# Key transposes of odd blocks moved to partitions 64 to 127 and issued in turn with the query transposes

## The chip, the cores and the metric

One core of one Trainium2 chip runs the kernel. The metric is the device time of one execution in microseconds; the time before is 1073.29 us, the median of three runs (1073.01 to 1078.38 us).

## The reference, cut to what matters

Three layers follow one another: attention over chunks, a feed-forward layer with a smooth activation, and a mixture of eight experts with one expert per token. The change touches the attention alone. Each chunk of 32 queries sees 8 memory keys, 16 keys to its left, its own 32 and 8 to its right:

```python
batch, n_heads, seq, head_dim = (4, 8, 768, 64)
for c in range(nc):
    q_c = q[:, :, c_start:c_end]
    k_ctx = k[:, :, l_start:r_end]
    k_full = np.concatenate([mem_k, k_ctx], axis=2)
    scores = scale * np.matmul(q_c, k_full.transpose(0, 1, 3, 2))
    ...
    out[:, :, c_start:c_end] = np.matmul(a, v_full)
```

The scores contract over the head dimension, so queries and keys have to lie with the head dimension on the partitions. They arrive from memory with the position on the partitions, and TensorE transposes them.

## The kernel before, in words

The attention is cut into 48 blocks of 64 queries and all 8 heads (u = 0 to 47, 12 blocks to a sequence). Blocks 0 to 17 are made by `blocks`, blocks 18 to 47 by `chunks` (line 1600, `BY_CHUNK` = 18). Blocks go in pairs that share one tile of transposed keys, kT. The even block of a pair loads its 64 queries and 96 keys (8 of memory, 24 of context, 64). The odd block loads 64 queries and the 64 keys that the even one has not brought.

For a block, the load (`load_qk`, lines 544 to 557) puts queries in qn, partitions 0 to 63, and keys in kn, from partition 0 on. The job T (lines 581 to 592) then makes eight transposes on TensorE, each of two heads (128 columns): first four of the queries into the PSUM tile p_qT (line 586), then four of the keys into the PSUM tile p_kT (line 588). p_qT and p_kT are two of three buffers of one tag, "a". The jobs qT and kT (lines 594 to 603) copy them to SBUF on ScalarE or VectorE, S (lines 605 to 617) makes the scores, and the softmax, PT (transposes of the weights), V (weights times values, lines 654 to 663) and the copies xh and xl follow.

The feed-forward layer runs at the same time: step s of `mlp` has a job mm_h (line 748, twelve matmuls) and a job mm_y (line 794, nine matmuls), with a chain of ScalarE and VectorE operations between them. Attention blocks are slipped in between these jobs, ahead of the feed-forward steps that need them. After the last rows the experts' stage follows (lines 1342 to 1522).

The order of the work is not written out by hand. Every job states its engines with a cost in ns (`job`, line 117), what it comes after and which buffers it takes, and `Plan.order` (lines 136 to 195) plays the program through on these costs: at each step it takes, among the jobs that could begin within `SLACK` = 34 ns of the earliest, the one of lowest rank. The engines then run the order so found, each its own queue in sequence. The cost of T on TensorE stands in line 683:

```python
job(("T", u), T, {E: 560 if odd else 630}, rank=R(0), after=[("qk", u)], ...
```

The loads are issued by SyncE (SP) in its own planned order; qn and kn have one buffer each, so a block's load waits for the T of the block before it.

Of the kernel before, what the change touches and what calls it, by code (L numbers as in the profile page):

```python
# [9 lines left out]
F32 = mybir.dt.float32  # L10
# [9 lines left out]
B, H, S, D = 4, 8, 768, 64  # L20
NMEM = 8
CHUNK, LEFT, RIGHT = 32, 16, 8
QB = 64
CTX = QB + LEFT + RIGHT
NK = CTX + NMEM
# [85 lines left out]
class Plan:  # L111
# [5 lines left out]
    def job(self, key, fn, on, rank, after=(), get=(), use=(), lat=130, tiled=False):  # L117
        uses = list(use) + [h for _, h in get]
        for h in uses:
            self.users.setdefault(h, []).append(key)  # L120
        for _, h in get:
            self.getter[h] = key
        self.jobs[key] = dict(fn=fn, on=on, rank=rank, after=list(after), get=list(get), use=list(use), lat=lat, tiled=tiled,
                              need=[(tag, sum(t == tag for t, _ in get)) for tag in dict(get)])
# [91 lines left out]
def attn_moe_moe_kernel(ctx, tc, q, k, v, mem_k, mem_v, w_in, w_out, emb, tau, w1, w2, cst, out, ydbg=None):  # L216
    nc = tc.nc
# [5 lines left out]
    ident = cf[:, 0:128]  # L223
# [10 lines left out]
    att = pa.enter_context(tc.tile_pool(name="att", bufs=1))  # L234
# [8 lines left out]
    def psa(shape, name):  # L243
        return ps_a.tile(shape, F32, tag="a", name=name)
# [3 lines left out]
    job, A, V_, G, E = plan.job, "Activation", "DVE", "Pool", "PE"  # L248
    engs = {A: nc.scalar, V_: nc.vector, G: nc.gpsimd}
    xt, yp = {}, {}  # L250
    tl = {}
# [278 lines left out]
    def chunks(u):  # L530
        b, i = divmod(u, NQB)
        j, o = divmod(u, SPB)
        R = lambda x: x + (1.4 * u - 17.5 if u < (LEAVE + 1) * SPB else 2 * o + 32 if j == LEAVE + 1 else 8 * u / 3 - 20.4)
        J = H // 2
        odd, pair = u % 2, u // 2
        w = QB * i - LEFT
        edge = 0 if i == 0 else 1 if i == NQB - 1 else None
        new = QB if odd else NMEM + PREV + QB
# [4 lines left out]

        def load_qk(e):
            qn = tl["qn", u] = att.tile([QB, H, D], F32, tag="qn", bufs=1, name="qn")
            kn = tl["kn", u] = att.tile([NK, H, D], F32, tag="kn", bufs=1, name="kn")
            get = lambda n, x, lo, hi: nc.sync.dma_start(out=kn[n:n + hi - lo], in_=x[b, :, lo:hi, :].rearrange("h p d -> p h d"))
            nc.sync.dma_start(out=qn, in_=q[b, :, i * QB:(i + 1) * QB, :].rearrange("h p d -> p h d"))
            if not odd:
                get(0, mem_k, 0, NMEM)  # L550
            lo, hi = w + (PREV if odd else 0), w + PREV + QB
            n = 0 if odd else NMEM
            if lo < 0:
                get(n, k, 0, -lo)
            if hi > NQB * QB:
                get(n + NQB * QB - lo, k, 0, hi - NQB * QB)
            get(n + max(-lo, 0), k, max(lo, 0), min(hi, NQB * QB))
# [23 lines left out]
        def T(e):  # L581
            p1 = psa([128, J, QB], "p_qT")
            p2 = psa([128, J, new], "p_kT")
            a, c = tl["qn", u], tl["kn", u]
            for n in range(J):
                nc.tensor.transpose(p1[:, n, :], a[:, 2 * n:2 * n + 2, :].rearrange("p h d -> p (h d)"), ident[:QB, :QB])
            for n in range(J):
                nc.tensor.transpose(p2[:, n, :], c[0:new, 2 * n:2 * n + 2, :].rearrange("p h d -> p (h d)"), ident[:new, :new])
            tl["T", u] = p1, p2
            tl["qT", u] = att.tile([128, J, QB], F32, tag="qT", name="qT")  # L590
            if not odd:
                tl["kT", pair] = att.tile([128, J, 5 * GR - NMEM], F32, tag="kT", name="kT")
# [78 lines left out]
        def x_lo(e):  # L671
# [4 lines left out]
        prev = lambda x: [(x, u - 1)]  # L676
        mem = 4 if u < BY_CHUNK + 2 or i < 2 else 0
        plan.dma(("qk", u), load_qk, dict(SP=470 * ((2 if odd else 3) + (edge is not None))), (QB + new) * 4e3, R(-4), [("issue", "qk", u - 1)], [(t, (t, u)) for t in ("qn", "kn")])
        plan.dma(("v", u), load_v, dict(SP=470 * (8 + mem + (2 if edge is not None else 0))), 4 * SEEN * 2e3, R(0), [("issue", "v", u - 1)], [("vn", ("vn", u))])
        t1, t2 = ("a", u, 1), ("a", u, 2)  # L680
        pss, pr, mxh, sm = ("pS", u), ("pr", u), ("mx", u), ("sm", u)
        kt, xb = ("kT", pair), [("X", u), ("X2", u)]
        job(("T", u), T, {E: 560 if odd else 630}, rank=R(0), after=[("qk", u)], use=[(t, u) for t in ("qn", "kn")] + ([kt] if odd else []),
            get=[("a", t1), ("a", t2), ("qT", ("qT", u))] + ([] if odd else [("kT", kt)]))
        job(("qT", u), qT, {A: 264, V_: 330}, rank=R(1), after=[("T", u)], use=[t1, ("qT", u)])
        job(("kT", u), kT, {A: 264, V_: 330} if odd else {A: 371 + 210, V_: 465 + 200}, rank=R(1), after=[("T", u)], use=[t2, kt])
# [253 lines left out]
    def routing():  # L940
# [51 lines left out]
        def group(g):  # L992
# [203 lines left out]
            for x, (j0, j1) in enumerate(chunks):  # L1196
                h = ("rhs", g, x)
                sh = [128, j1 - j0, ns]
                wd = 60 + (j1 - j0) * ns
                cc = slice(j0, j1)  # L1200

                def ids(e, x=x, sh=sh, cc=cc, h=h):
                    if g == 2:
                        p = gp if ctag[x][0] == "g" else mp
                        t = r[h] = p.tile([128, CH, 6, ns], BF16, tag=ctag[x], bufs=1 if x > 5 else 2, name="rhs2")
                    else:
                        t = r[h] = r["rhs1"][x]
                    V.tensor_tensor(t[:, :, 0, :], mid(slots[g], sh), last(r["z"][:, cc], sh), ALU.is_equal)

                key = ("ids", g, x)  # L1210
                job(key, ids, {V_: wd}, rank=rk, after=[k3] + ([("mm_y", KFF * NBLK - 1)] if g == 2 else []), use=every,
                    get=[(ctag[x], h)] if g == 2 else [])
                us = [h] if g == 2 else []
                ch.append((j0, j1, h, us))
                last_ids.append(steps([
                    ({V_: wd}, lambda e, h=h: e.tensor_scalar(r[h][:, :, 1, :], r[h][:, :, 0, :], part, None, ALU.mult)),
                    ({V_: wd}, lambda e, h=h, sh=sh, cc=cc: e.tensor_tensor(r[h][:, :, 2, :], r[h][:, :, 0, :], last(tiles[:, cc], sh), ALU.mult)),
                ], [key], rk, us))
                last_gates.append(steps([
                    ({V_: wd}, lambda e, h=h, m=m, sh=sh, cc=cc: e.tensor_tensor(r[h][:, :, 3 + m, :], r[h][:, :, 0, :], last(r["gb"][m][:, cc], sh), ALU.mult))  # L1220
                    for m in range(3)
                ], [last_ids[-1], gate], rk + (2 if g == 1 else 30), us))
# [376 lines left out]
    for u in range(NSUB):  # L1599
        (blocks if u < BY_CHUNK else chunks)(u)  # L1600
# [7 lines left out]
    for kind, n in TURNS:  # L1608
        c = FIRST + 2 * n
# [50 lines left out]
```

## Time and profile before

| | us |
|---|---|
| median of three runs | 1073.29 |
| the profiled execution | 1077.64 |
| its span, first to last instruction | 1075.9 |
| TensorE busy | 1044.6 |
| VectorE busy | 751.5 |
| ScalarE busy | 692.2 |
| GpSimd busy | 168.0 |

The profiled execution is 4.35 us above the median. The span is what the rows of the trace divide up; the profiled execution's time is 1.74 us longer than it. PE stands for TensorE's matmuls, PEld for its weight loads, which can run beside matmuls; a transpose is a weight load of the data and a matmul with the identity. DVE is VectorE, ACT is ScalarE, SP is SyncE. A row of the timeline merges neighbouring instructions of one line: start, length from the first start to the last end, count. The ends of matmuls are modelled, so starts say more than ends.

### The profile page before, as it was taken

The numbers are of one execution on the slowest core, as the hardware profiler recorded it, in microseconds if no ns is written. First come the engines' busy times: TensorE is split into PE (matmuls) and PEld (weight loads), VectorE is DVE, ScalarE is ACT, GpSimd is POOL, SyncE is SP. The second block draws the span as 40 slices with busy tenths as digits, with TensorE's granted clock in tenths as the row PEclk, the third lists the DMA queues.
The fourth block names the chain that finished last, engine by engine and source line by source line (L and its number), as shares of the span: only waits on it lengthen the run. The fifth ranks groups of instructions, "written<-read, shape, count | busy, mean of one in ns | idle before, by whom it ended". The sixth has DMA issues, their size and how long they took to land. (4 is left out here: it accounts for less than half of the span.)

```text
span 1075.9 us, 22578 instructions
## 1 busy us (share of the span) xinstructions
PE 1044.6 (97%) x8404; PEld 912.3 (85%) x8404; DVE 751.5 (70%) x1607; ACT 692.2 (64%) x1617; POOL 168.0 (16%) x109
## 2 busy tenths in 40 slices
PE   8899999999999999999999999998999999999996
PEld 6678888998888888888888889888899888988995
DVE  5999996556756566556556556886978657777851
ACT  4888887777757777777777777855633444443441
POOL 0000100000000000000000000010135645655552
PEclk9899999999999999999999999998999999999998
DMA  7966540032331112112112100019459877568200
GB/s 192 258 195 183 160 128 23 1 101 62 97 80 40 41 41 60 40 43 61 41 40 70 28 17 31 1 27 378 173 188 399 292 227 250 170 216 268 88 30 22
DMA packets 164019, 128.09 MB, mean 119 GB/s; under 512 B 106229, under 2 KB 135285, under 8 KB 163647
## 3 DMA queue, kind: packets, MB, share of 16 engines
q1 hardware_dynamic: 159439, 111.63, 34.4%
q0 software_dynamic: 4464, 14.95, 3.9%
q8 instruction: 69, 1.13, 0.4%
q14 instruction: 47, 0.39, 0.1%
HBM read 119.19 MB, written 16.52 MB: 126 GB/s over the span
## 5 line engine op out<-in xcount | busy, mean ns | idle before, releaser
L748 PE MATMUL p_h<-xt,win_h 128*128 128x384 f32 x1024 | 273.3, 348 | 1.7 <-DVE rn L777 1.5
L748 PEld LDWEIGHTS p_h<-xt,win_h 128*128 128x128 f32 x1024 | 183.0, 190 | 9.4 <-DVE rn L777 3.2
L748 PE MATMUL p_h<-xt,win_l 128*128 128x384 f32 x512 | 174.2, 340 | 0.0
L767 DVE SCALAR_TENSOR_TENSOR m<-sq,rn 128x384 f32<-128x384 f32 x128 | 71.8, 561 | 123.1 <-ACT rn L256 122.4
L794 PE MATMUL p_y<-wout_h,gh 128*128 128x512 f32 x384 | 155.9, 406 | 0.5 <-DVE gh L266 0.5
L266 ACT CAST ehi<-eraw 128x1024 fp32r<-128x1024 f32 x89 | 92.8, 1048 | 98.5 <-PE p_y L1496 51.5
L1378 DVE TENSOR_TENSOR elo<-eraw,ehi 128x1024 fp32r<-128x1024 f32 x89 | 125.6, 1419 | 42.6 <-ACT ehi L266 35.8
L794 PE MATMUL p_y<-wout_h,gl 128*128 128x512 f32 x384 | 151.8, 395 | 0.0
L794 PE MATMUL p_y<-wout_l,gh 128*128 128x512 f32 x384 | 151.4, 394 | 0.0
L1496 PE MATMUL p_y<-ehi,hh 128*128 128x512 f32 x432 | 142.1, 398 | 1.0 <-DVE hh L1465 1.0
L1406 PE MATMUL p_h<-xs,ehi 128*128 128x256 f32 x704 | 129.5, 285 | 0.0
L752 ACT ACTIVATE sq<-p_h 128x384 f32<-128x384 f32 x128 | 62.4, 488 | 78.4 <-PE p_h L748 78.0
L1406 PEld LDWEIGHTS p_h<-xs,ehi 128*128 128x128 f32 x704 | 111.0, 191 | 1.6 <-DVE xs L1359 0.4
L1378 POOL TENSOR_TENSOR elo<-eraw,ehi 128x1024 fp32r<-128x1024 f32 x39 | 96.9, 2484 | 79.8 <-ACT ehi L266 51.7
L1406 PE MATMUL p_h<-xs,elo 128*128 128x256 f32 x352 | 100.4, 285 | 0.0
L771 ACT ACTIVATE m<-m,few 128x384 f32<-128x384 f32 x128 | 79.1, 618 | 32.1 <-DVE m L767 31.2
L1300 POOL DMA_INDIRECT vn<-y_d,gi x27 | 27.6, 1023 | 453.3 <-DVE si L1247 402.7
L1496 PEld LDWEIGHTS p_y<-ehi,hh 128*128 128x128 f32 x432 | 81.1, 188 | 19.6 <-DVE hh L1465 2.3
L748 PEld LDWEIGHTS p_h<-xt,win_l 128*128 128x128 f32 x512 | 97.0, 190 | 0.0
L794 PEld LDWEIGHTS p_y<-wout_h,gl 128*128 128x128 f32 x384 | 72.2, 188 | 17.7 <-DVE gl L785 0.4
L1496 PE MATMUL p_y<-elo,hh 128*128 128x512 f32 x216 | 85.3, 395 | 0.0
L774 DVE SCALAR_TENSOR_TENSOR rn<-m,rn 128x384 f32<-128x384 f32 x128 | 70.8, 553 | 20.4 <-ACT m L771 19.1
(285 smaller groups left out, 1872.3 us busy)
## 6 DMA issues: line engine op xcount, KB each, us to landing
eraw<-in_moe_w_dram SPq DMA_DIRECT2D x128, 512.0 KB
raw<-in_moe_w_in_dram SPq DMA_DIRECT2D x16, 512.0 KB
raw<-in_moe_w_out_dram SPq DMA_DIRECT2D x16, 512.0 KB
y_d<-ysb SPq DMA_DIRECT2D x24, 256.0 KB
qn<-in_q_dram SPq DMA_DIRECT2D x43, 128.0 KB
vn<-in_v_dram SPq DMA_DIRECT2D x114, 32.0 KB
vn<-in_v_dram SPq DMA_DIRECT2D x122, 24.0 KB
kn<-in_k_dram SPq DMA_DIRECT2D x22, 128.0 KB
```

Of the source, the lines that this page charges most:

```text
L266: (nc.scalar.copy if e == A else nc.vector.tensor_copy)(out, src)
L748: nc.tensor.matmul(p, w, xt[j][:, a, kk, :], start=(n == 0), stop=(n == len(ops) - 1))
L752: nc.scalar.activation(t, tl["h", s], AF.Tanh, scale=0.5)
L767: nc.vector.scalar_tensor_tensor(t, tl["sq", s], 4.0, tl["rn", s], ALU.add, ALU.mult)
L771: nc.scalar.activation(t, t, AF.Square, bias=c15)
L774: nc.vector.scalar_tensor_tensor(tl["rn", s], tl["m", s], 0.75, tl["rn", s], ALU.add, ALU.mult)
L794: nc.tensor.matmul(yp[yh][t], x[:, c], w[g][:, o, :], start=(first and n == 0), stop=(final and n == 2))
L1300: nc.gpsimd.indirect_dma_start(out=tl["xg", u, a], out_offset=None, in_=y_d[0:T1 * 128, :] if g == 1 else y_d[:, :], in_offset=bass.Indire ...
L1378: engs[e].tensor_sub(tl["elo", j], raw[b, second, c], tl["ehi", j].bitcast(F32))
L1406: nc.tensor.matmul(p[:, o, :], w[:, kk, s], v[:, kk, :], start=(kk == 0 and m == 0), stop=(kk == KDM - 1 and m == 2))
L1496: nc.tensor.matmul(tl["yy", u][a], v[:, kk, s], w[:, k, :], start=(kk == 0 and m == 0), stop=(kk == KEF - 1 and m == 2))
```

## The change

In `chunks`, that is for blocks 18 to 47: the keys of odd blocks are loaded to partitions 64 to 127 of kn (which now has 128 partitions instead of 96), and their transposes read them there, with that corner of the identity. The two loops over transposes become one, so that queries and keys take turns, in odd blocks and in even blocks alike; the keys of even blocks stay where they were. The planner's cost of T in odd blocks goes from 560 to 330 ns; that in even blocks stays at 630.

```diff
-            kn = tl["kn", u] = att.tile([NK, H, D], F32, tag="kn", bufs=1, name="kn")
+            kn = tl["kn", u] = att.tile([128, H, D], F32, tag="kn", bufs=1, name="kn")
...
-            n = 0 if odd else NMEM
+            n = QB if odd else NMEM
...
             a, c = tl["qn", u], tl["kn", u]
+
+            r = slice(QB, QB + new) if odd else slice(0, new)
             for n in range(J):
                 nc.tensor.transpose(p1[:, n, :], a[:, 2 * n:2 * n + 2, :].rearrange("p h d -> p (h d)"), ident[:QB, :QB])
-            for n in range(J):
-                nc.tensor.transpose(p2[:, n, :], c[0:new, 2 * n:2 * n + 2, :].rearrange("p h d -> p (h d)"), ident[:new, :new])
+                nc.tensor.transpose(p2[:, n, :], c[r, 2 * n:2 * n + 2, :].rearrange("p h d -> p (h d)"), ident[r, r])
...
-        job(("T", u), T, {E: 560 if odd else 630}, rank=R(0), ...
+        job(("T", u), T, {E: 330 if odd else 630}, rank=R(0), ...
```

## Rows read from the trace of the kernel before

**Rows 1.** The page: busy time by engine; TensorE's busy tenths and granted clock.

```profile
PE 1044.6 (97%) x8404; PEld 912.3 (85%) x8404; DVE 751.5 (70%) x1607; ACT 692.2 (64%) x1617; POOL 168.0 (16%) x109
...
PE   8899999999999999999999999998999999999996
...
PEclk9899999999999999999999999998999999999998
```

**Rows 2.** Windows: stretch, length, busy by engine (instructions), PEclk, DMA share, GB/s.

```profile
150.00:615.00 465.00, 459.63 (x4182) 397.45 (x4181) 292.88 (x707) 345.11 (x914) 1.36 (x2) 0.99 0.21 53
615.00:1076.00 461.00, 444.85 (x2955) 398.39 (x2953) 323.08 (x589) 231.74 (x368) 157.44 (x95) 0.98 0.47 162
```

**Rows 3.** Waits of TensorE's matmuls in 150 to 615 us: total, times, longest.

```profile
PE p_S L616 <- ACT kT L266: 3.8, 2, 2.1
PE p_h L748 <- DVE rn L777: 1.0, 3, 0.4
PE p_PT L646 <- DVE lg L892: 0.3, 1, 0.3
PE p_yT L854 <- ACT kT L266: 0.2, 1, 0.2
```

**Rows 4.** Lines 586 and 588: duration min/median/max, first and last start, forms.

```profile
L586 PE MATMUL p_qT<-cf,qn x120: 221/222/365, 153.4 to 612.2; 64*128 64x64 f32 x120
...
L588 PE MATMUL p_kT<-cf,kn x120: 221/246/311, 153.7 to 612.5; 96*128 96x96 f32 x60, 64*128 64x64 f32 x60
```

**Rows 5.** Groups of TensorE by line and shape: count, busy us, mean ns.

```profile
L586 PE MATMUL p_qT<-cf,qn 64*128 64x64 f32 x120 | 13.9, 237 | 0.0
...
L588 PE MATMUL p_kT<-cf,kn 96*128 96x96 f32 x60 | 8.2, 260 | 0.0
L588 PE MATMUL p_kT<-cf,kn 64*128 64x64 f32 x60 | 6.3, 228 | 0.0
```

**Rows 6.** Timeline of PE about an odd block's T: start us, length us.

```profile
271.72 0.38 PE L646 MATMUL p_PT<-cf,pr 128*128 128x128 f32 x2
272.03 0.46 PE L586 MATMUL p_qT<-cf,qn 64*128 64x64 f32 x4
272.33 0.41 PE L588 MATMUL p_kT<-cf,kn 64*128 64x64 f32 x4
272.67 0.62 PE L748 MATMUL p_h<-xt,win_h 128*128 128x384 f32 x2
```

**Rows 7.** Timeline of PE about an even block's T.

```profile
260.80 0.38 PE L646 MATMUL p_PT<-cf,pr 128*128 128x128 f32 x2
261.11 0.46 PE L586 MATMUL p_qT<-cf,qn 64*128 64x64 f32 x4
261.50 0.55 PE L588 MATMUL p_kT<-cf,kn 96*128 96x96 f32 x4
261.83 0.60 PE L748 MATMUL p_h<-xt,win_h 128*128 128x384 f32 x2
```

**Rows 8.** Timeline of PEld about the even, then the odd T: key weights.

```profile
261.50 0.36 PEld L588 LDWEIGHTS p_kT<-cf,kn 96*128 96x128 f32 x4
...
272.27 0.33 PEld L588 LDWEIGHTS p_kT<-cf,kn 64*128 64x128 f32 x4
```

**Rows 9.** Timeline of PE: a block's V, whose matmuls use quarters of the array in turn.

```profile
293.56 0.67 PE L662 MATMUL p_X<-pT,vn 64*64 64x32 f32 x32
```

**Rows 10.** Timeline of PE: the second T of this stage, at 162 us.

```profile
162.18 0.69 PE L586 MATMUL p_qT<-cf,qn 64*128 64x64 f32 x4
162.66 0.63 PE L588 MATMUL p_kT<-cf,kn 64*128 64x64 f32 x4
165.41 0.65 PE L616 MATMUL p_S<-kT,qT 64*32 64x64 f32 x32 [2.12 <-ACT kT L266]
```

**Rows 11.** Windows of 10 us, columns as in rows 2.

```profile
150.00:160.00 10.00, 8.26 (x75) 7.03 (x74) 10.00 (x21) 9.61 (x22) 0.00 (x0) 0.99 0.49 134
160.00:170.00 10.00, 7.88 (x62) 7.07 (x61) 9.04 (x33) 8.43 (x31) 0.00 (x0) 0.67 0.21 59
...
260.00:270.00 10.00, 10.00 (x114) 8.67 (x113) 5.65 (x16) 7.43 (x26) 0.00 (x0) 1.00 0.27 60
```

**Rows 12.** Timeline of PE: another even block, its T and its S.

```profile
243.60 0.46 PE L586 MATMUL p_qT<-cf,qn 64*128 64x64 f32 x4
243.99 0.55 PE L588 MATMUL p_kT<-cf,kn 96*128 96x96 f32 x4
...
246.90 0.65 PE L616 MATMUL p_S<-kT,qT 64*32 64x64 f32 x32
```

**Rows 13.** Waits of the copies of p_qT, and of SP's queue, 150 to 615 us.

```profile
ACT qT L256 <- PE p_qT L586: 0.9, 1, 0.9
...
SPq L548 <- PE p_kT L588: 36.5, 18, 6.4
```

More of the change, by code (lines that the diff above doesn't have):

```diff
@@ L682, in chunks @@
         kt, xb = ("kT", pair), [("X", u), ("X2", u)]
-        job(("T", u), T, {E: 560 if odd else 630}, rank=R(0), after=[("qk", u)], use=[(t, u) for t in ("qn", "kn")] + ([kt] if odd else []),
+        job(("T", u), T, {E: 330 if odd else 630}, rank=R(0), after=[("qk", u)], use=[(t, u) for t in ("qn", "kn")] + ([kt] if odd else []),
             get=[("a", t1), ("a", t2), ("qT", ("qT", u))] + ([] if odd else [("kT", kt)]))
```

## The prediction
> **What bounds the kernel now.** First the page: TensorE is busy 97% of the span, the other engines 70% or less, and its row of tenths has no hole but at the ends [rows 1]. Then the windows: the T jobs that the change touches lie between 153.4 and 612.5 us [rows 4], and in the stretch that holds them TensorE is busy 459.6 of 465 us [rows 2]. Then its waits there: they add up to 5.3 us, 3.8 of them in two waits of S [rows 3]. So here TensorE's own queue sets the pace; a nanosecond added to or taken from it moves everything behind it, and the experts' stage after it, also TensorE's (444.9 of 461 us [rows 2]), begins by so much later or sooner. What has to be priced is T itself, 120 query and 120 key transposes in 30 blocks, 15 odd and 15 even [rows 4].
>
> **What T costs now, step by step.** In an odd block queries and keys have the same shape, 64 rows by 128 columns. The four key transposes last 0.41 us together, one lasts 0.222 (the median), so three steps take 0.19: 0.063 each [rows 4, 6]. From the first query to the first key it is 0.30 us, four such steps and 0.05 in which the first query waits for its own weights [rows 6].
>
> In an even block the keys have 96 rows. Now it is 0.39 us from the first query to the first key, 0.09 more than in the odd one [rows 6, 7]. And the first key takes longer than the others: the mean is 260 ns, the median 246, and with one long one in four that makes it 4 x 14 = 56 ns [rows 4, 5]. The weights say why: in the odd block the first key's load begins at 272.27, 0.06 ahead of its matmul, beside the last queries; in the even block load and matmul are both at 261.50, after the queries are out [rows 6 to 8]. **A change of the array's shape from 64 to 96 rows so costs 0.09 + 0.056 = 0.145 us.** The way back is seen at each T's start: the second of two 128-row transposes begins at about 260.80 + 0.38 - 0.27 = 260.91, its plain step is 0.11, yet the first query comes 0.20 after it: 0.09 more, and the 0.05 of its own weights, 0.14 to 0.145 again [rows 7]. From 96 to 128 rows there is no such hole (261.50 to 261.83 is four steps of 0.083) [rows 7]; from 64 to 128 there is (272.33 to 272.67, 0.34 for four steps of 0.063) [rows 6].
>
> The Trainium skill ("TensorEngine Tiling (Array Packing)", section "Key Properties") speaks against the change here: it says that a change of tiling mode, not of the tile alone, drains the engine. It names no price; by the rule alone the sum would only get its sign for the even blocks. The trace agrees with it at 0.145 us a change.
>
> **The change, part by part.** *Even blocks: the turns.* One merged loop puts a 64-row query before each 96-row key, so the shape changes 8 times in a T (once in, four times to the keys, three times back) where it now changes twice. Six more at 0.145 are 0.87 us, and 15 even blocks make **+13.0 us**. Nothing hides this: it lies in TensorE's own queue. A single step from 96 to 64 rows isn't in the trace; its bounds are nothing (the step from 96 to 128 rows) and 0.145 (128 to 64), and I take 0.145, since the narrow shape is entered in both. With the lower end the even blocks cost half, +6.5 us.
>
> *Odd blocks: side by side.* Queries on partitions 0 to 63 and keys on 64 to 127 use the two halves of the array's rows. No transposes stand side by side in the trace. The nearest row is V, whose 32 matmuls take turns over row and column halves and write to two PSUM tiles, as the new T does: 0.67 us in all, less one matmul of about 0.22 is 0.45 us for 31 steps, 0.0145 each, four beside one another in what a T step takes [rows 9]. So I take a query and a key in one step of 0.063: four steps fewer, 0.25 us per odd block. The block at 162 us runs at the lower clock, with steps of (0.63 - 0.31) / 3 = 0.106, and saves 0.42 [rows 4, 10]. In sum 14 x 0.25 + 0.42, **-3.9 us**. Bounds: nothing, if two loads of all 128 columns can't run together (V's loads have 64), and -3.9; I take the full saving.
>
> *Loads.* As many DMAs with as many bytes, to other partitions, and kn has still one buffer. SP's load of the next block's queries and keys waits for the last key transpose (18 times, 36.5 us in all) [rows 13], so it comes 0.87 us later behind an even T and 0.25 sooner behind an odd one, as TensorE does; none of TensorE's waits in the stretch is for a load [rows 3]. Zero.
>
> *Copies.* The last query transpose now comes next to last: in an even block it moves from 0.23 to about 1.35 us after T's start, 0.24 more than TensorE's own delay. ScalarE or VectorE may stand that much longer at qT (such a wait is seen once, 0.9 us [rows 13]), and what is queued behind, links of the feed-forward chain, comes later; TensorE waits for that chain 1.0 us in the whole stretch [rows 3]. S follows T by 3.3 us [rows 12] and the copies fit into this. I take zero, with up to +2 us in the range (half of the 15 by 0.24).
>
> *The planner.* The odd T's cost falls by 230 ns, which is close to what I expect (0.25), the even one's stays at 630, now 0.87 us too little. Order may change from the second T on. No row shows the new order; the waits that a bad or good order makes are of the size of the 5.3 us in rows 3, some of which can vanish or come again. I take zero and +-2.5 us for the range.
>
> **Sum.** +13.0 - 3.9 = +9.1 us. Against the profiled execution of 1077.64 us that is 1086.7. The runs shown have a median of 1073.29, 4.35 lower; the edit is counted in steps that don't depend on this, so the forecast is 1073.29 + 9.1 = **1082.4 us**, 0.85% slower. Measurements of this kernel can tell about 0.5% from no change, that is 1067.9 to 1078.7 us.
>
> **Rivals.** *Even blocks lose nothing (the other side).* If a matmul that stands alone between two changes lets the next weights load beside it, the turns are free, and the odd saving is left: 1073.29 - 3.9 = 1069.4, within 0.5%. For it: steps from 96 to 128 rows show no hole [rows 7]. Against it: both directions between 64 and more rows show one each time. It decides at 3.9 / 90 = 0.043 us a change, where the sum is zero; over 0.103 us the result is slower by 0.5%. At half price (only the way to the keys) it is +2.6: 1075.9, within 0.5% as well. 11 in 100.
>
> *Odd transposes don't run together.* Then only the +13.0 is left: 1086.3. For it: each loads all 128 columns, V's only 64. 10 in 100.
>
> *Order.* The planner's new order adds waits such as those of S for kT, 3.8 us more [rows 3]: 1086.2; or takes them away: 1078.6. 10 in 100, split evenly.
>
> *The clock.* In 160 to 170 us it was granted 0.67 of full speed, after a stretch in which TensorE was busy 8.3 of 10 us; with levels of 1.2 and 2.4 GHz this is 6.6 us at the lower one, 3.3 us lost [rows 11]. A long even T is a stretch with holes; if it made the clock fall three times, +9.9 on top: 1092.3. Against it: 260 to 270, with an even T and all else, is at 1.00 [rows 11]. The Trainium skill ("TensorE: Matmul & The Clock Gate", section "Part 4: PE-mode transpose") says that the full clock doesn't engage for transposes; by that rule a T of 1.6 us between matmuls would be likelier to bring a fall. The medians of 222 and 246 ns [rows 4] are those of T at full speed [rows 6, 7], and longer ones belong to the one T of [rows 10], so 5 in 100.
>
> **How the numbers follow.** The forecast has 64 in 100, with its own range from 1079 to 1086. All cases but the first rival and half of the order's lie over 1078.7. Slower by over 0.5%: 0.84; within: 0.13; faster, which needs the odd saving, free turns and a better order together: 0.03. The range leaves out most of the first rival and of the clock's: 1076.5 to 1088.5 us.
>
> **What would show it.** Right: in even blocks the timeline has single query and key transposes about 0.2 us apart, T from first query to the next job grows from 0.72 to about 1.6 us; in odd blocks it shrinks from 0.64 to about 0.39; TensorE's waits stay near 5 us and the span grows by 9. Wrong: even T under 1.1 us long, odd T still over 0.6, the lower clock in slices between 150 and 615 us that have it not now, or new waits of S or of the feed-forward matmuls over 3 us.

## The result, and the profile after

The changed kernel takes 1084.82 us, the median of six runs, where the kernel before takes 1073.46 beside it: 11.4 us more, a ratio of 1.0104 with a 95% interval of 1.0085 to 1.0123. It is slower; the forecast was 1082.4 us, +9.1.

TensorE's timeline about an even block's T comes first (start us, length us), the answer to [rows 7]. Line 586 (queries) is line 588 in the changed kernel; from line 588 (keys) on, every line number is one higher.

```profile
260.31 0.27 PE L588 MATMUL p_qT<-cf,qn 64*128 64x64 f32 x1
260.51 0.30 PE L589 MATMUL p_kT<-cf,kn 96*128 96x96 f32 x1
260.75 0.27 PE L588 MATMUL p_qT<-cf,qn 64*128 64x64 f32 x1
260.95 0.30 PE L589 MATMUL p_kT<-cf,kn 96*128 96x96 f32 x1
...
261.82 0.30 PE L589 MATMUL p_kT<-cf,kn 96*128 96x96 f32 x1
261.90 0.42 PE L749 MATMUL p_h<-xt,win_h 128*128 128x384 f32 x1
```

Each transpose now stands 0.20 to 0.24 us behind the one before, where neighbours of one shape stood 0.06 to 0.08 apart. From the first query to the next job it is 261.90 - 260.31 = 1.59 us; it was 0.72 [rows 7]. That is 0.87 us more, 13.0 us over 15 blocks. The weight loads of the same stretch start only with their matmuls:

```profile
260.51 0.14 PEld L589 LDWEIGHTS p_kT<-cf,kn 96*128 96x128 f32 x1
260.75 0.14 PEld L588 LDWEIGHTS p_qT<-cf,qn 64*128 64x128 f32 x1
```

The same view about an odd block's T, against [rows 6]:

```profile
272.09 0.27 PE L588 MATMUL p_qT<-cf,qn 64*128 64x64 f32 x1
272.10 0.27 PE L589 MATMUL p_kT<-cf,kn 64*128 64x64 f32 x1
272.20 0.22 PE L588 MATMUL p_qT<-cf,qn 64*128 64x64 f32 x1
272.21 0.22 PE L589 MATMUL p_kT<-cf,kn 64*128 64x64 f32 x1
...
272.48 0.44 PE L749 MATMUL p_h<-xt,win_h 128*128 128x384 f32 x1
```

A query and a key start within 0.01 us of each other; a pair takes the step of one. T goes from 0.64 to 0.39 us, 0.25 less: 3.8 us over 15 blocks.

The groups of TensorE by line and shape (count, busy us, mean ns) show it over all 30 blocks, beside [rows 5]:

```profile
L588 PE MATMUL p_qT<-cf,qn 64*128 64x64 f32 x120 | 23.2, 253 | 0.0
L589 PE MATMUL p_kT<-cf,kn 96*128 96x96 f32 x60 | 18.1, 302 | 0.0
L589 PE MATMUL p_kT<-cf,kn 64*128 64x64 f32 x60 | 6.9, 235 | 0.0
```

Before, only the first key of each four was 56 ns longer, which made a mean of 260. Now the mean is 302: every single key of an even block waits for its own weights.

TensorE's waits between 150 and 628 us (total, times, longest), against [rows 3]:

```profile
PE p_S L617 <- ACT kT L266: 4.0, 2, 2.9
PE p_yT L855 <- ACT pT L266: 1.7, 2, 0.8
PE p_yT L855 <- DVE yt L867: 1.0, 1, 1.0
PE p_yT L855 <- ACT kT L266: 0.9, 1, 0.9
PE p_PT L647 <- DVE lg L893: 0.3, 1, 0.3
PE p_h L749 <- DVE rn L778: 0.2, 1, 0.2
```

They add up to 8.1 us instead of 5.3. The new ones belong to line 855, which transposes finished rows for the routing. Its jobs now stand elsewhere in the order: the planner, with a shorter odd T on its books, puts such a job ahead of an mm_h three times (at 420, 509 and 597 us), and the waits of those three make up the 1.7 and the 1.0 us above. The first of these places in the timeline:

```profile
418.83 0.44 PE L647 MATMUL p_PT<-cf,pr 128*128 128x128 f32 x2
420.26 0.63 PE L855 MATMUL p_yT<-cf,ysb 128*128 128x128 f32 x4 [0.99 <-DVE yt L867]
420.65 0.48 PE L795 MATMUL p_y<-wout_h,gh 128*128 128x512 f32 x1
```

The clock isn't part of the loss; in these two executions it hides a part of it. The windows (stretch, length, busy by engine, granted clock, DMA share, GB/s), beside [rows 2, 11]:

```profile
150.00:628.00 478.00, 469.88 (x4206) 400.14 (x4208) 293.73 (x705) 351.22 (x927) 1.36 (x2) 1.00 0.20 52
160.00:170.00 10.00, 7.13 (x65) 6.26 (x64) 9.79 (x39) 8.75 (x32) 0.00 (x0) 0.83 0.22 61
```

From 160 to 170 us the granted clock is 0.83 where it was 0.67, which at the levels of 1.2 and 2.4 GHz is 1.7 us lost instead of 3.3. The window of the whole stretch, with the fifteen long T in it, is at 1.00.

All in all T accounts for +13.0 - 3.8 = +9.2 us and the waits for +2.8: 12.0 us, against 11.4 measured and an interval of 9.1 to 13.2.

### The profile page after: what moved, and what is told of

Its sections match the earlier page's. It is cut to its first block, busy times and chain, and to the rows that moved or that the text cites. A ratio compares the mean times of both kernels' runs of the same rounds, so it can differ in the third digit from the quotient of the medians.

```text
span 1082.7 us, 22577 instructions
## 1 busy us (share of the span) xinstructions
PE 1051.6 (97%) x8404; PEld 914.0 (84%) x8404; DVE 750.8 (69%) x1601; ACT 695.0 (64%) x1623; POOL 170.6 (16%) x109
## 5 line engine op out<-in xcount | busy, mean ns | idle before, releaser
L1379 DVE TENSOR_TENSOR elo<-eraw,ehi 128x1024 fp32r<-128x1024 f32 x89 | 130.8, 1478 | 39.9 <-ACT ehi L266 39.6
L795 PEld LDWEIGHTS p_y<-wout_h,gh 128*128 128x128 f32 x384 | 72.3, 188 | 13.6 <-DVE gh L266 0.9
```

What stands on the lines that cost most here:

```text
L795: nc.tensor.matmul(yp[yh][t], x[:, c], w[g][:, o, :], start=(first and n == 0), stop=(final and n == 2))
L1379: engs[e].tensor_sub(tl["elo", j], raw[b, second, c], tl["ehi", j].bitcast(F32))
```

## The experiments

The theory: each change between a 64-row and a wider transpose costs 0.145 us of TensorE's own time, side-by-side pairs save 0.25 us per odd block, and what else there is comes as waits from the order. The rivals: the turns themselves cost (another tile, another PSUM bank), the late copies behind an even T cost, or the pairs save nothing that arrives. Times of single runs of one kernel differ by some 10 us, so beside each ratio stands a second measure from the profiled execution: the stage of the changed T jobs, from the first to the last query transpose. It is 612.2 - 153.4 = 458.8 us in the kernel before [rows 4] and 622.9 - 152.8 = 470.1 in the changed one, +11.3. (The span as a whole grew less, from 1075.9 to 1082.7 us: outside the stage the profiled execution of the kernel before, which lies 4.35 us over the median, took 617.1 us and that of the changed kernel 612.6.)

The clock enters this second measure. By what the granted clock lacks of 1 between 150 and 180 us, times the length, the lower level cost about 3.4 us there in the profiled execution of the kernel before and in five others; in those of the changed kernel, odd blocks alone, even blocks alone, the cost of before and one shape with both parts it cost 1.7, and in the last of the table nothing. By this estimate the stage of those five would stand 1.7 us higher against before at equal clock, that of the last 3.4. For the changed kernel this is 13.0 us, 1 us over T and waits; where that 1 us went was not found.

| | time, us against before (95% interval) | stage, us against before | TensorE's waits 150 to 628, us |
|---|---|---|---|
| before | | | 5.3 |
| changed | +11.2 (9.1 to 13.2) | +11.3 | 8.1 |
| odd blocks alone | -1.4 (-3.2 to 0.4) | -2.6 | 7.0 |
| even blocks alone | +12.5 (9.6 to 15.5) | +11.3 | 5.2 |
| changed, cost of before | +10.4 (8.3 to 12.6) | +9.8 | 6.6 |
| new cost alone | +2.0 (0.1 to 4.1) | +2.0 | 7.0 |
| even by twos | +1.6 (0.2 to 3.1) | +4.2 | 5.3 |
| odd alone, new cost | +0.8 (-1.0 to 2.4) | +0.3 | 8.3 |
| one shape, both parts | -6.3 (-8.8 to -3.9) | -5.0 | 7.4 |
| one shape in even blocks alone | -2.8 (-4.3 to -1.3) | -2.2 | 6.0 |
| even in halves | -4.8 (-6.7 to -3.0) | -4.2 | 6.6 |
| changed, true even cost | +10.3 (7.7 to 12.9) | +9.2 | 7.5 |

The first column is the ratio less one, times the 1073.5 us of before, so it can differ by 1 us from the difference of the medians.

**Odd blocks alone.** Turns only where `odd`, keys of odd blocks on partitions 64 to 127, costs of before:

```diff
-            for n in range(J):
-                nc.tensor.transpose(p1[:, n, :], ...)
-            for n in range(J):
-                nc.tensor.transpose(p2[:, n, :], c[0:new, ...
+            turns = [x for n in range(J) for x in ((0, n), (1, n))] if odd else [(x, n) for x in range(2) for n in range(J)]
+            for x, n in turns:
+                ...
```

> Turns and partitions 64 to 127 in odd blocks alone, planner's costs of before. If each turn from 64 to 96 rows costs 0.145 us and pairs run side by side: odd T from first query to the next job 0.39 us instead of 0.64, even T as before at 0.72, time 15 x 0.25 = 3.7 us under the kernel before (about 1069.8). If the odd blocks' gain is eaten elsewhere (copies, loads): within 1 us of before.

Measured: 1071.99 us beside 1073.31, ratio 0.9987 (0.997 to 1.0004). Each odd T is 0.39 us long as expected, yet less than the 3.7 us arrives. The waits say where part of it goes:

```profile
PE p_S L620 <- ACT kT L266: 4.4, 2, 2.7
PE p_h L752 <- DVE rn L781: 1.4, 4, 0.5
PE p_yT L858 <- ACT kT L266: 0.9, 1, 0.9
```

TensorE comes sooner to jobs that wait for ScalarE or VectorE, and stands there: 7.0 us instead of 5.3. At 163.51 us, S waits 2.72 us for the copy of keys where it waited 2.12 [rows 10]:

```profile
163.51 0.48 PE L620 MATMUL p_S<-kT,qT 64*32 64x64 f32 x20 [2.72 <-ACT kT L266]
```

In the kernel before, the T ahead of it ran at the lower clock [rows 10, 11]. Two later versions have the full clock at this T: even blocks alone, where it has its old length, and the changed kernel with the cost of before, where it has the new one.

```profile
163.57 1.08 PE L620 MATMUL p_S<-kT,qT 64*32 64x64 f32 x32 [2.62 <-ACT kT L266]
163.59 0.65 PE L617 MATMUL p_S<-kT,qT 64*32 64x64 f32 x32 [2.88 <-ACT kT L266]
```

The 0.25 us that this T saves are lost again at once in the wait behind it. Over the stage it is -3.8 + 1.7 = -2.1 us; the interval holds this, but not -3.7. The stage itself has -2.6, and -0.9 at equal clock, which the interval holds as well.

**Even blocks alone.** The same with `if not odd`, odd keys where they were.

> Turns in even blocks alone, planner's costs of before. If the shape changes are the whole loss: even T 1.59 us instead of 0.72, time 13.0 us over before (about 1086.5). If the late copies behind an even T cost TensorE something of their own: 15 us or more over before.

Measured: 1086.62 us beside 1073.31, ratio 1.0116 (1.0089 to 1.0144). An even T takes 1.59 us and TensorE's waits stay at 5.2 us, so the copies that come later cost it nothing. The whole loss is in the even T. (At equal clock the stage has these 13.0 us too.)

**The changed kernel with the cost of before, and the new cost alone.** One number each: line 684 of the changed kernel, as shown, and line 683 of the kernel before, the other way round:

```diff
-        job(("T", u), T, {E: 330 if odd else 630}, ...
+        job(("T", u), T, {E: 560 if odd else 630}, ...
```

> The changed kernel with the planner's cost of the odd T back at 560, so with the order of before. If the new order costs about 2 us (new waits of the row transposes, line 855): about 9.2 us over before (1082.6). If the order is worth nothing: 11.4 us over before, as the changed kernel (1084.8).

> The kernel before with the planner's cost of the odd T at 330 and nothing else, so with the order of the changed kernel. If the order costs about 2 us: 1075.5. If it is worth nothing by itself: 1073.5, within 1 us of before.

Measured: 1083.55 (ratio 1.0097, 1.0077 to 1.0117) and 1076.04 us (1.0019, 1.0001 to 1.0038) beside 1073.31. The new cost alone, with T itself as before, costs about 2 us, and brings the two waits that the order of before doesn't have; TensorE's jobs stand in the same order in its trace as in that of the changed kernel:

```profile
PE p_yT L854 <- ACT pT L266: 1.6, 2, 0.8
...
PE p_yT L854 <- DVE yt L866: 1.0, 1, 1.0
```

With the cost of before the changed kernel loses them, 1.3 us by the medians. The intervals of the two versions of the changed kernel overlap; the waits are what tells them apart. Of its 2.8 us of new waits 1.5 go with the order (8.1 to 6.6); 1.3 stay (6.6 to 5.3) and belong to the odd blocks' pairs, since even blocks alone have 5.2.

**Odd blocks alone with the new cost.** The first experiment with 330.

> Odd blocks alone as in the first experiment, with the planner's cost at 330, so with the order of the changed kernel. If odd pairs save 3.7 us and the new order costs 1.5 to 2: 1071.3 to 1071.8. If the lower cost fits the odd T and the order is at no loss then: 1069.8.

Measured: 1074.54 us beside 1073.46, ratio 1.0007 (0.9991 to 1.0022), with waits of 8.3 us. Neither expectation holds: even the order's 2 us and the pairs' 3.7 leave a gain by the first, and none was seen. The waits account for it, -3.8 + 3.0 = -0.8 us, within the interval. The part of the change that is sound by itself gains nothing that can be measured when the planner is told of it.

**Even by twos.** Two queries, two keys, two queries, two keys; odd blocks and costs of before. The line is set against that of even blocks alone:

```diff
-            turns = [x for n in range(J) for x in ((0, n), (1, n))] if not odd else ...
+            turns = [(x, 2 * m + n) for m in range(2) for x in range(2) for n in range(2)] if not odd else ...
```

> Even blocks in the order two queries, two keys, two queries, two keys; odd blocks and costs of before. If each change of shape costs 0.145 us: two more in each even T, 0.72 + 0.29 = 1.01 us, 15 x 0.29 = 4.4 us over before (1077.8). If the loss belongs to a matmul that stands alone between two changes: under 1.5 us over before.

Measured: 1076.02 us beside 1073.46, ratio 1.0015 (1.0002 to 1.0029).

```profile
243.96 0.33 PE L590 MATMUL p_qT<-cf,qn 64*128 64x64 f32 x2
244.22 0.38 PE L592 MATMUL p_kT<-cf,kn 96*128 96x96 f32 x2
244.54 0.33 PE L590 MATMUL p_qT<-cf,qn 64*128 64x64 f32 x2
244.80 0.38 PE L592 MATMUL p_kT<-cf,kn 96*128 96x96 f32 x2
244.97 0.42 PE L752 MATMUL p_h<-xt,win_h 128*128 128x384 f32 x1
```

T is 244.97 - 243.96 = 1.01 us, 0.29 over [rows 7] for two more changes: 0.145 each, as expected, whether or not a transpose stands alone between changes. The stage has +4.2 us; the timed runs show less, +1.6 with at most 3.1. A part of the difference is the clock: these runs had a mean granted clock of 0.9898, those of the kernel before beside them 0.9881, and over all timed runs 0.001 of it goes with about 0.7 us (an estimate, from the spread of times and clocks within each kernel's runs), so 1.2 us here. The rest was not found.

**One shape in even blocks.** Even blocks load 96 queries, the 32 of the next block's half for nothing, and transpose them with 96 rows; otherwise the changed kernel with the costs of before.

```diff
-            qn = tl["qn", u] = att.tile([QB, H, D], F32, tag="qn", bufs=1, name="qn")
+            nq = QB if odd else new
+            qn = tl["qn", u] = att.tile([new, H, D], F32, tag="qn", bufs=1, name="qn")
...
-                nc.tensor.transpose(p1[:, n, :], a[:, 2 * n:2 * n + 2, :].rearrange("p h d -> p (h d)"), ident[:QB, :QB])
+                nc.tensor.transpose(p1[:, n, :], a[0:nq, 2 * n:2 * n + 2, :].rearrange("p h d -> p (h d)"), ident[:nq, :nq])
```

> The changed kernel, costs of before, but even blocks load 96 queries and transpose them with 96 rows (32 of them for nothing), so that query and key turns have one shape. If it is the change of shape that costs: no 0.145 us holes in an even T, which goes from first query to the next job in 8 x 0.083 + 0.05 = 0.7 us without the hole at its entry; time 3.7 us (odd) + 15 x 0.1 us (even) under before at most, 1068.5 to 1072. If it is the turns themselves (other tile, other PSUM bank): an even T of about 1.6 us and 9 us over before.

Measured: 1068.24 us beside 1073.46, ratio 0.9941 (0.9918 to 0.9964).

```profile
259.25 0.38 PE L649 MATMUL p_PT<-cf,pr 128*128 128x128 f32 x2
259.47 0.25 PE L590 MATMUL p_qT<-cf,qn 96*128 96x96 f32 x1
259.55 0.24 PE L591 MATMUL p_kT<-cf,kn 96*128 96x96 f32 x1
259.63 0.24 PE L590 MATMUL p_qT<-cf,qn 96*128 96x96 f32 x1
...
260.07 0.60 PE L751 MATMUL p_h<-xt,win_h 128*128 128x384 f32 x2
```

The turns are still there, to other tiles and other PSUM buffers, and the holes are gone: steps of 0.08, and the first query 0.11 us behind the last 128-row transpose instead of 0.20. So it is the change of shape that costs, not taking turns; and the change from 128 to 96 rows costs nothing. T is 0.60 us long, less than the 0.7 expected. Per even block it saves both changes of before and pays 0.02 us more for each query: 0.29 - 4 x 0.02 = 0.21 us, 3.1 us in 15 blocks; I had expected at most 1.5 because I counted one of the two changes. This version beats both kernels.

**The same without the odd blocks' pairs,** queries first and then keys, costs of before.

> Even blocks with 96 queries (one shape, queries first, then keys), odd blocks and costs of before. One hole less at the entry of an even T, about 0.11 us, 15 times: 1.6 us under before (1071.8). If the odd blocks' side-by-side pairs are worth 3.7 us, the kernel with both (1068.2) is that much under this one; if they are worth 1.3 us only, as the first experiment's median has it, this one comes out at about 1069.5.

Measured: 1071.45 us beside 1073.9, ratio 0.9974 (0.996 to 0.9988). With 3.1 us in T and 0.7 of new waits, -2.4 us was due. Against the version with both parts it leaves about 2.8 us for the odd pairs, by the two differences of medians (5.2 and 2.4). Two more comparisons differ in the pairs alone: even blocks alone against the changed kernel with the cost of before (1086.62 and 1083.55) has 3.1 us, the new cost without and with them (+2.7 and +1.1) has 1.6. With the first experiment's 1.3, all four are less than 3.7.

**Even in halves.** The even block's 96 keys as 64 on partitions 64 to 127 and 32 that are packed by halves of the heads on partitions 0 to 63, ten transposes of 64 rows, four pairs; three more DMAs and one more copy.

```diff
-                get(0, mem_k, 0, NMEM)
+                few_ = lambda n, x, lo, hi: nc.sync.dma_start(out=kn[CHUNK * c + n:CHUNK * c + n + hi - lo, 0:H // 2], ...
...
+            for m in range(0 if odd else 2):
+                nc.tensor.transpose(px.rearrange("p (a m) w -> p m a w", m=2)[:, m], c[0:QB, 2 * m:2 * m + 2, :]..., ident[:QB, :QB])
```

> Odd blocks as in the changed kernel, costs of before; the 96 keys of an even block cut into 64 on partitions 64 to 127 and 32 that are packed by head halves on partitions 0 to 63, so that its ten transposes all have 64 rows and four pairs run side by side. Even T: 6 steps of 0.062 and a way out of 0.15 + 0.1, 0.18 us less than before each, 2.7 us; with the odd blocks 3.7 us more: 1067. It costs three more DMAs and one more copy of an even block; if those are felt, over 1070.

Measured: 1068.72 us beside 1073.46, ratio 0.9955 (0.9938 to 0.9972). T is 0.51 us long (242.84 to 243.35 in the timeline below) instead of 0.72, and 1.3 us of new waits take part of it back. It is no better than the simpler version.

```profile
242.84 0.27 PE L590 MATMUL p_qT<-cf,qn 64*128 64x64 f32 x1
242.85 0.27 PE L591 MATMUL p_kT<-cf,kn 64*128 64x64 f32 x1
...
243.14 0.28 PE L594 MATMUL p_qT<-cf,kn 64*128 64x64 f32 x2
243.35 0.62 PE L755 MATMUL p_h<-xt,win_h 128*128 128x384 f32 x2
```

**The changed kernel with the true cost of an even T,** `{E: 330 if odd else 1500}`.

> The changed kernel with the planner's cost of an even T at 1500 instead of 630, near what it takes. If the 1 to 2 us that the changed kernel is over the sum of its steps come from the planner not knowing of the long even T: its new waits go, 1083 or less. If any new order costs about as much, or the rest is chance: 1084 to 1086.

Measured: 1084.36 us beside 1073.9, ratio 1.0096 (1.0072 to 1.012). The waits of line 855 are others but not gone (7.5 us in all). It can't be told from the changed kernel: that the planner didn't know of the long T is not shown to cost anything.

## Why the prediction was right

*Even blocks:* right to the step. The two bounds for the way from 96 to 64 rows were nothing and 0.145 us; the measured T of 1.59 us is what 0.145 gives, and even blocks by twos confirm it. Taking the upper bound was an argument there and no measurement. The prediction says that a single step from 96 to 64 rows isn't in the trace, but there is one in the part that the change leaves alone, at 20 us, from matmuls of 64 columns to transposes of 128:

```profile
20.17 0.69 PE L489 MATMUL p_X<-pT,vn 96*64 96x64 f32 x16
20.79 0.46 PE L410 MATMUL p_qT<-cf,qkn 64*128 64x64 f32 x4
```

The last of the sixteen begins at about 20.17 + 0.69 - 0.22 = 20.64 and the query 0.15 behind it: 0.09 over a plain step of 0.06, as on the way to the keys [rows 7]. This spoke against the lower bound of nothing. The four steps of 0.083 behind the first key [rows 7] are an average: in the trace they are 0.14, 0.08, 0.08 and 0.03, which leaves the length of T and so the sum as it is.

The Trainium skill says that a change of tiling mode drains the engine ("TensorEngine Tiling (Array Packing)", section "Key Properties"). The trace agrees for 64 against 96 rows, at 0.145 us a change, with weights that load only with their own matmul.

*Odd blocks:* T shrank by 0.25 us as V's row had suggested, although each transposes all 128 columns. That this arrives in full was the weak part: of 3.8 us in T, 1.3 to 3.1 arrived by the medians of four comparisons, and TensorE waited 1.3 to 1.7 us more for ScalarE and VectorE. The 0.42 us that the prediction counted for the T at 162 us hung on the clock of one execution: in the changed kernel's this T ran at full clock.

*The terms that were off* are the planner's, which I put at zero within 2.5 us, and the odd blocks' saving, which I took in full. The new order brought 1.5 us of new waits and the pairs 1.3, together 2.8; the forecast of +9.1 lies 2.3 under the measured 11.4, at the lower end of its interval, so the times alone don't show that it was too low. The waits do: the sign that they stay near 5 us did not come true (8.1). The rival of the order was right in its direction; new waits of 1.5 us, and 2 us for the cost alone, are about half of its 3.8, and they came not at S for kT but at the row transposes of line 855.

*Loads, copies, clock:* the loads cost nothing. ScalarE did wait longer for queries, 4.0 us in six waits where it was 0.9 in one [rows 13]:

```profile
ACT qT L256 <- PE p_qT L588: 4.0, 6, 1.0
```

TensorE lost nothing by it, as even blocks alone show. The clock fell no more often than before (0.83 from 160 to 170 us, 1.00 over the whole stretch), so its rival did not come true. The rule of the Trainium skill that spoke for it, that the full clock doesn't engage for transposes ("TensorE: Matmul & The Clock Gate", section "Part 4: PE-mode transpose"), found no support in a T of 1.6 us between matmuls; a longer stretch of transposes alone was not run.

## What to carry to other kernels

When two small matmul streams are merged to run side by side, look at every place that shares the merged loop: here taking turns paid where both had 64 rows on different halves of the partitions, and cost 0.145 us at each turn between 64 and 96 rows. Shapes can be made equal with rows that are thrown away; eight transposes of 96 rows beat four of 64 and four of 96. And a planner that gets a truer cost for one job may place others worse: measure the order by itself.

## What the runs showed that I had not expected

Side-by-side transposes cost nothing at all beside one another: a 64-row query and key start 0.01 us apart and both last 0.22 us, as one did alone. And of the 3.8 us that the pairs saved on TensorE, the bound engine at 97% of the span, only 1.3 to 3.1 arrived: even there a shorter job can end in a wait for another engine.
